# An attention block with a token and channel mixer on one core: all weight pieces converted during the attention steps, the second channel weight read back in 12 pieces

## The chip, the cores and the metric

One core of a Trainium2 chip runs the whole program. The metric is the device time of one execution in microseconds (us), and of several runs the median. The engines are called by the profile's names: PE is TensorE (PEld its weight loads), DVE is VectorE, ACT is ScalarE, POOL is GpSimd, and SP issues most of the DMA transfers.

## The reference

Windowed causal attention over 8 batches of 8 heads, followed by a mixer over tokens and a mixer over channels. Everything is float32.

```python
# q, k, v: (8, 8, 576, 64)
scores = (q @ k^T) / 8;  key position p is seen by position t if 0 <= t - p < 64
attn   = exp(scores - max) / (sum + 1e-9)
x      = (attn @ v) as (8, 576, 512)
u      = x + (relu(x^T @ w_tok1) @ w_tok2)^T      # w_tok1 (576, 256), w_tok2 (256, 576)
out    = u + relu(u @ w_ch1) @ w_ch2              # w_ch1 (512, 1536), w_ch2 (1536, 512)
```

The four weights are float64. They reach the chip as 64-bit words and are made float32 there, with integer and float operations on DVE. Products with weights are computed in three passes: each operand is split into a rounded part (hi) and a rest (lo), and hi x hi, hi x lo and lo x hi are summed.

## The kernel before

**Attention steps.** The 576 rows of each batch are cut into 9 blocks of 64. A tile holds two such blocks for all 8 heads, and there are 36 tiles, 9 to a pair of batches. The loop of lines 433 to 505 runs over i = -1 to 36 and is software-pipelined. Step i issues, in this order: the scores of tile i+1 (`qk`, L239 on PE), the transposition of the first half of tile i's probabilities (`pt_transpose`, L274 on PE, copied by ACT at L276), the mask and row maximum of the first half of tile i+1 (`softmax`, L256 and L259 on DVE), the exponentials (`softmax_exp`, L267 on ACT), a piece of the second token layer (`tok2`, L365 to L377), the second halves of the same, the first token layer for the tile before (`tok1`, L330), the value product (`av`, L286) and its normalisation (`norm`, L300 on DVE, result `x`). `split_x` then makes hi and lo of `x` on ACT and POOL for the first token layer. In the prediction, step i is the stretch from the scores of tile i+1 to those of tile i+2.

**Weight conversions.** The weights are converted in 39 jobs: 4 pieces of 320 columns of w_tok1, 3 of 384 of w_tok2, 16 of 384 of w_ch1 (jobs 7 to 22) and 16 of 384 of w_ch2 (jobs 23 to 38). A job has a load (tile `raw`, three buffers), a first half on DVE (`to_f32_a`, L162 to L164, writes `c`), a second half on DVE (`to_f32_b`, L173 to L176, writes `r`), and an addition on POOL (L178, writes `w`). `c` and `w` have two buffers, `r` has one. In the step after, `job_finish` splits the result: for w_ch1 an ACT cast to `w1hi` and a POOL subtraction to `w1lo` (L89 and L92 inside `split`). For w_ch2 it stores `w` to a scratch tensor in HBM, `w2_dram`, because the on-chip memory that w_ch2 will occupy still belongs to the attention. The table `JOBS` says how many conversions a step takes; a step that is not in it takes one, or none where i % 9 is 5. No loads are issued from step 34 on. So 33 jobs are converted in the attention steps, and the last six pieces of w_ch2 are not.

**Channel stage.** The 4608 tokens are cut into 9 chunks of 512. For chunk j the first layer computes 12 output tiles `gp` of 12 matmuls each (L549), which ACT and DVE evict as `ghi` and `glo` (L553, L554); then the second layer computes four tiles `op` of 36 matmuls (L583), adds `uf` and stores. `gp` has four PSUM tiles in turn. In chunk 0, after each output tile, `split_w2` splits a piece of w_ch2 that was read back from `w2_dram` (ACT cast to `w2hi`, POOL subtraction to `w2lo`), `load_w2` starts the next read (two buffers, pieces of 512 columns, the last of 256), and one of the six late jobs moves on: `job_finish`, `job_convert_a`, `job_convert_b` and a load.

**What sets the order.** Nothing is scheduled by a program: each engine runs its instructions in the order in which the code issues them, and the semaphores of the tile framework make them wait for data and buffers. All loads named here stand in SP's queue.

Of the kernel before, what the change touches and what calls it, by code (L numbers as in the profile page):

```python
# [10 lines left out]
F32 = mybir.dt.float32  # L11
F32R = mybir.dt.float32r
I32 = mybir.dt.int32
U32 = mybir.dt.uint32
I64 = mybir.dt.int64
# [6 lines left out]
C = H * D  # L22
P = 128
# [3 lines left out]
TPP = 9  # L27
# [4 lines left out]
NFT = F // P  # L32
# [3 lines left out]
CW = 384  # L36
# [36 lines left out]
def mixer_kernel(ctx: ExitStack, tc: tile.TileContext, qh, kh, vh, wt1, wt2, wc1, wc2, out):  # L73
    nc = tc.nc
# [12 lines left out]
    def split(eng_hi, eng_lo, hi, lo, src):  # L87
        if eng_hi is nc.scalar:
            nc.scalar.copy(hi, src)  # L89
        else:  # L90
            eng_hi.tensor_copy(hi, src)
        eng_lo.tensor_sub(lo, src, hi.bitcast(F32))  # L92
# [15 lines left out]
    with ExitStack() as actx:  # L108
# [3 lines left out]

        mask = [pa.tile([P, P], F32, name=f"mask{m}") for m in range(2)]

        kbs, loaded, cpool = {}, {}, [pq]

        def load_k(i):
            p, t = divmod(i, TPP)
# [37 lines left out]
        def to_f32_a(raw, n, tag):  # L156

            words = raw[:, :n].bitcast(I32).rearrange("p (n t) -> p n t", t=2)
            low, high = words[:, :, 0], words[:, :, 1]
            c = cpool[0].tile([P, CW], I32, name=f"c{tag}", tag="cvc", bufs=2)[:, :n]  # L160
            cf = c.bitcast(F32)
            nc.vector.tensor_scalar(out=c, in0=high, scalar1=0x7FFFFFFF, scalar2=None, op0=ALU.bitwise_and)  # L162
            nc.vector.tensor_scalar(out=cf, in0=cf, scalar1=F64_LOW, scalar2=F64_HIGH, op0=ALU.max, op1=ALU.min)
            nc.vector.tensor_scalar(out=c, in0=c, scalar1=3, scalar2=0x3FFFFFFF,  # L164
                                    op0=ALU.logical_shift_left, op1=ALU.bitwise_and)
            return c, low, high, n, tag

        def to_f32_b(c, low, high, n, tag):

            r = cpool[0].tile([P, CW], I32, name=f"r{tag}", tag="cvr", bufs=1)[:, :n]  # L170
            w = cpool[0].tile([P, CW], F32, name=f"w{tag}", tag="cvw", bufs=2)[:, :n]
            cf, rf = c.bitcast(F32), r.bitcast(F32)
            nc.vector.scalar_tensor_tensor(out=c, in0=high, scalar=-0x40000000, in1=c,  # L173
                                           op0=ALU.bitwise_and, op1=ALU.bitwise_or)
            nc.vector.tensor_scalar(out=r, in0=c, scalar1=-0x800000, scalar2=None, op0=ALU.bitwise_and)
            nc.vector.scalar_tensor_tensor(out=rf, in0=low.bitcast(U32), scalar=2.0 ** -52, in1=rf,  # L176
                                           op0=ALU.mult, op1=ALU.mult)
            nc.gpsimd.tensor_add(w, rf, cf)  # L178
            return w
# [8 lines left out]
        def job_load():  # L188
            if to_load:
                n = to_load.pop(0)  # L190
                src, _, _, o, m = jobs[n]
                raw = cpool[0].tile([P, CW], I64, name=f"raw{n}", tag="raw", bufs=3 if cpool[0] is pq else 2)
                nc.sync.dma_start(raw[:, :m], src[:, o:o + m])
                to_convert.append((n, raw))

        to_convert_b = []

        def job_convert_a():
            if to_convert:
                n, raw = to_convert.pop(0)  # L200
                to_convert_b.append((n, to_f32_a(raw, jobs[n][4], n)))

        def job_convert_b():
            if to_convert_b:
                n, part = to_convert_b.pop(0)
                to_finish.append((n, to_f32_b(*part)))
# [226 lines left out]
        for i in range(-1, NT + 1):  # L433
# [76 lines left out]
    with ExitStack() as bctx:  # L510
# [1 line left out]
        w2hi = pb.tile([P, NFT, C], F32R, name="w2hi")  # L512
        w2lo = pb.tile([P, NFT, C], F32R, name="w2lo")

        w2hf, w2lf = (t.rearrange("p f c -> p (f c)") for t in (w2hi, w2lo))
        cpool[0] = pb
        n_early = jobs[to_load[0]][3] if to_load else NFT * C
        early = [(o, min(C, n_early - o)) for o in range(0, n_early, C)]
        w2_raw = {}

        def load_w2():
            if early:
                o, m = early.pop(0)
                w2_raw[o, m] = pb.tile([P, C], F32, name=f"raww2_{o}", tag="raww2", bufs=2)
                nc.sync.dma_start(w2_raw[o, m][:, :m], w2_dram[:, o:o + m])

        def split_w2():
            if w2_raw:
                (o, m), raw = next(iter(w2_raw.items()))
                del w2_raw[o, m]  # L530
                split(nc.scalar, nc.gpsimd, w2hf[:, o:o + m], w2lf[:, o:o + m], raw[:, :m])

        load_w2()
        load_w2()
        late = list(to_load)
        while to_load and len(to_convert) < 2:
            job_load()
        for n in late:
            jobs[n] = (wc2, w2hf, w2lf) + jobs[n][3:]

        for j in range(NCHUNK):
            uf, uhi, ulo = ul.pop(j)
            g = []
            for ft in range(NFT):
                gp = ps.tile([P, CHUNK], F32, name=f"gp{j}_{ft}", tag=("s", "pt")[ft % 2])
                k = 0
                for ct in range(NCT):
                    for w, x in ((w1hi, uhi), (w1hi, ulo), (w1lo, uhi)):
                        nc.tensor.matmul(gp, w[:, ct * F + ft * P:ct * F + (ft + 1) * P], x[:, ct], start=(k == 0), stop=(k == 3 * NCT - 1))  # L549
# [4 lines left out]
                nc.vector.scalar_tensor_tensor(out=glo, in0=gp, scalar=0.0, in1=ghi.bitcast(F32),  # L554
                                               op0=ALU.max, op1=ALU.subtract)
                g.append((ghi, glo))
                if j == 0:
                    job_finish()
                    split_w2()
                    load_w2()  # L560
                    job_convert_a()
                    job_convert_b()
                    while to_load and len(to_convert) < 2:
                        job_load()
                if ft == 3 and j + 1 < NCHUNK:
                    ul[j + 1] = load_u(j + 1, pu)
                if ft == 8 and j + 1 < NCHUNK:
                    split_u(ul[j + 1])
# [56 lines left out]
```

## Time and profile before

| | us |
|---|---|
| median of 3 runs | 903.66 (903.43 to 905.66) |
| profiled execution | 901.16 |
| its span, first to last instruction | 899.2 |
| PE busy | 871.6 (97%) |
| DVE busy | 381.5 (42%) |
| ACT busy | 305.0 (34%) |
| POOL busy | 129.5 (14%) |

The attention steps with the token mixer end at 290.17 us of the span, when the first `gp` matmul's row begins; the channel stage takes the rest. The shares of busy time are averages over these two: DVE is busy nine tenths of the time in much of the attention and about two tenths in the channel stage. A matmul's end is modelled and its start overlaps the one before, so a PE that shows busy may still be held up a little, and the length of a stretch of the chain says more than its busy share. The granted TensorE clock is 0.997 on average.

### The profile page before, as it was taken

How to read it: one execution, taken by the hardware profiler on the slowest of the kernel's cores; microseconds unless marked ns; L12 is line 12 of the kernel's file. 1: busy time of each engine (PE TensorE's matmuls, PEld its weight loads, DVE VectorE, ACT ScalarE, POOL GpSimd, SP SyncE). 2: the span in 40 equal slices, each digit the busy share in tenths (PEclk: the TensorE clock that was granted, in tenths of full speed). 3: DMA queues.
4: the chain of work that ended last, by engine and by line, in shares of the span. 5: the costliest groups of instructions: out<-in, count | busy, mean ns of one | idle time of the engine just before them, and what ended most of it. 6: DMA issues, size and time to landing. Idle time of an engine off the chain costs nothing.

```text
span 899.2 us, 14591 instructions
## 1 busy us (share of the span) xinstructions
PE 871.6 (97%) x6002; PEld 704.7 (78%) x6002; DVE 381.5 (42%) x686; ACT 305.0 (34%) x953; POOL 129.5 (14%) x130
## 2 busy tenths in 40 slices
PE   7889999999999989999999999999999999999998
PEld 5667777778878768888888888888888888888887
DVE  5989979988883870130220220230220220220210
ACT  5777778787774240120120120120120220210210
POOL 2434434443331540000000000000000000000000
PEclk9999999999999999999999999999999999999999
DMA  9666668578636420100100100100100100100001
GB/s 325 183 209 237 218 216 269 184 230 293 213 124 206 113 92 36 58 1 36 59 0 36 59 1 36 58 1 36 59 12 24 59 13 23 59 12 36 0 12 36
DMA packets 41490, 87.05 MB, mean 97 GB/s; under 512 B 5456, under 2 KB 19408, under 8 KB 39504
## 3 DMA queue, kind: packets, MB, share of 16 engines
q1 hardware_dynamic: 39312, 84.29, 28.2%
q10 hardware_dynamic: 2112, 1.84, 0.6%
q8 instruction: 47, 0.77, 0.4%
q14 instruction: 19, 0.16, 0.1%
HBM read 65.27 MB, written 20.84 MB: 96 GB/s over the span
## 4 chain that ended last, share of the span: by engine, by line
PE 80%; DVE 14%; ACT 4%; issue 1%; DMA 0%; POOL 0%; SPq 0%; DVEq 0%; ACTq 0%
PE op L583 33%; PE gp L549 31%; PE up L372 4%; PE s L239 3%; PE xp L286 3%; PE h L330 3%; ACT e L267 2%; DVE nm L259 2%; DVE e L256 2%; PE up L365 2%; DVE c L173 2%; PE pp L274 1%; DVE c L162 1%; DVE c L164 1%; ACT pt L276 1%
## 5 line engine op out<-in xcount | busy, mean ns | idle before, releaser
L553 ACT ACTIVATE ghi<-gp 128x512 fp32r<-128x512 f32 x108 | 64.4, 598 | 462.6 <-PE gp L549 461.6
L549 PE MATMUL gp<-uhi,w1hi 128*128 128x512 f32 x432 | 170.5, 395 | 5.9 <-DVE glo L554 5.9
L549 PE MATMUL gp<-uhi,w1lo 128*128 128x512 f32 x432 | 172.9, 400 | 0.0
L549 PE MATMUL gp<-ulo,w1hi 128*128 128x512 f32 x432 | 171.0, 396 | 0.0
L583 PE MATMUL op<-glo,w2hi 128*128 128x512 f32 (+1 forms) x444 | 170.4, 384 | 0.0
L583 PE MATMUL op<-ghi,w2hi 128*128 128x512 f32 (+1 forms) x444 | 170.3, 384 | 0.0
L583 PE MATMUL op<-ghi,w2lo 128*128 128x512 f32 (+1 forms) x444 | 170.2, 383 | 0.0
L554 DVE SCALAR_TENSOR_TENSOR glo<-gp,ghi 128x512 fp32r<-128x512 f32 x108 | 74.4, 690 | 198.3 <-ACT ghi L553 198.2
L585 DVE TENSOR_TENSOR uf<-op,uf 128x512 f32<-128x512 f32 (+1 forms) x37 | 25.1, 677 | 262.7 <-PE op L583 262.7
L549 PEld LDWEIGHTS gp<-uhi,w1hi 128*128 128x128 f32 x432 | 81.5, 189 | 27.0 <-DVE glo L554 7.6
L267 ACT ACTIVATE e<-e,nm 128x128 f32<-128x128 f32 x232 | 90.4, 392 | 25.6 <-DVE nm L259 24.2
L549 PEld LDWEIGHTS gp<-ulo,w1hi 128*128 128x128 f32 x432 | 81.4, 188 | 20.8
L583 PEld LDWEIGHTS op<-ghi,w2hi 128*128 128x128 f32 x444 | 83.4, 188 | 16.7
L583 PEld LDWEIGHTS op<-ghi,w2lo 128*128 128x128 f32 x444 | 83.4, 188 | 16.5
L583 PEld LDWEIGHTS op<-glo,w2hi 128*128 128x128 f32 x444 | 83.4, 188 | 16.5
L549 PEld LDWEIGHTS gp<-uhi,w1lo 128*128 128x128 f32 x432 | 81.5, 189 | 18.9
L178 POOL TENSOR_TENSOR w<-r,c 128x384 f32<-128x384 f32 (+1 forms) x39 | 38.7, 993 | 142.3 <-DVE r L176 116.5
L286 PEld LDWEIGHTS xp<-v,pt 128*64 128x64 f32 x1152 | 39.4, 139 | 21.0 <-ACT pt L276 8.7
L286 PE MATMUL xp<-v,pt 128*64 128x64 f32 x1152 | 47.0, 229 | 5.8 <-ACT pt L276 5.0
L276 ACT COPY pt<-pp 128x512 f32<-128x512 f32 x72 | 41.7, 583 | 13.1 <-PE pp L274 12.8
L239 PE MATMUL s<-k,q 64*64 64x128 f32 x1152 | 43.3, 284 | 2.1 <-DVE c L173 1.6
L256 DVE SCALAR_TENSOR_TENSOR e<-s,mask 128x512 f32<-128x512 f32 x58 | 39.6, 683 | 13.2 <-PE s L239 13.1
(70 smaller groups left out, 1027.7 us busy)
## 6 DMA issues: line engine op xcount, KB each, us to landing
v<-vh SPq DMA_DIRECT2D x36, 512.0 KB, 4.2
raw<-wc SPq DMA_DIRECT2D x32, 384.0 KB, 4.5
q<-qh SPq DMA_DIRECT2D x36, 256.0 KB, 4.5
k<-kh SPq DMA_DIRECT2D x7, 1280.0 KB, 8.2
out<-uf SPq DMA_DIRECT2D x35, 256.0 KB, 2.3
uf<-u_dram SPq DMA_DIRECT2D x8, 1024.0 KB, 5.6
u_dram<-u SPq DMA_DIRECT2D x7, 512.0 KB, 4.4
w_dram<-w SPq DMA_DIRECT2D x10, 192.0 KB, 3.9
```

Of the source, the lines that this page charges most:

```text
L178: nc.gpsimd.tensor_add(w, rf, cf)
L239: nc.tensor.matmul(s[u][half * BLK:(half + 1) * BLK, j], qt[r, j, half], kbs[b][r, j, n * BLK:n * BLK + P], start=not on_pe, stop=True, sk ...
L256: nc.vector.scalar_tensor_tensor(out=e, in0=s_ps.pop((i, u)), scalar=scale, in1=mk.unsqueeze(1).to_broadcast([P, 4, P]), op0=ALU.mult, op1 ...
L267: nc.scalar.activation(e[:, h], src[:, h], AF.Exp, bias=nm[:, g:g + 1], scale=by, accum_out=sm[:, g:g + 1])
L276: nc.scalar.copy(pt, pp)
L286: nc.tensor.matmul(xp[half * BLK:(half + 1) * BLK, h], pts[h % 2][:, h // 2, half * BLK:(half + 1) * BLK], vt[:, half, h], start=True, sto ...
L330: nc.tensor.matmul(h_ps[b][tt], w[r, slot * DT + tt * P:slot * DT + (tt + 1) * P], x[r], start=first and n == 0, stop=last and n == len(co ...
L372: nc.tensor.matmul(up[:, :n], hx[:, cs], w[:, tt * S + s0:tt * S + s0 + n], start=False, stop=(k == 6), skip_group_check=True)
L549: nc.tensor.matmul(gp, w[:, ct * F + ft * P:ct * F + (ft + 1) * P], x[:, ct], start=(k == 0), stop=(k == 3 * NCT - 1))
L553: nc.scalar.activation(ghi, gp, AF.Relu)
L554: nc.vector.scalar_tensor_tensor(out=glo, in0=gp, scalar=0.0, in1=ghi.bitcast(F32), op0=ALU.max, op1=ALU.subtract)
L583: nc.tensor.matmul(op, w[:, ft, cs], x[:, cols], start=(k == 0), stop=(k == 3 * NFT - 1))
```

## The change

All 39 jobs are converted in the attention steps. `JOBS` now gives two conversions to steps 11, 16, 20, 25 and 29 and none to 34, 35 and 36; every other step takes one, also 6, 14, 23 and 32, which took none. Since the jobs run out after step 32, step 33 has none left. The late path goes: the loop that emptied the queue in step 35 becomes an assertion, and chunk 0 no longer loads, converts or finishes jobs. The conversion's tiles always come from the pool `pq`, so the list `cpool` goes too. w_ch2 comes back from `w2_dram` in 12 pieces of 512 columns instead of 7 and a half, with three buffers instead of two.

```diff
-JOBS = {-1: 1, 0: 1, 1: 1, 5: 1, 6: 0, 34: 1, 35: 1, 36: 0}
+JOBS = {11: 2, 16: 2, 20: 2, 25: 2, 29: 2, 34: 0, 35: 0, 36: 0}
...
-            n_jobs = JOBS.get(i, 1 if i % TPP != 5 else 0)
+            n_jobs = JOBS.get(i, 1)
...
             if i == NT - 1:
-                while to_convert or to_convert_b or to_finish:
-                    job_convert_a()
-                    job_convert_b()
-                    job_finish()
+                assert not (to_load or to_convert or to_convert_b or to_finish)
...
-        early = [(o, min(C, n_early - o)) for o in range(0, n_early, C)]
-        w2_raw = {}
+        w2_loads = [slice(ft, ft + 1) for ft in range(NFT)]
+        w2_raw = []
...
+                raw = pb.tile([P, C], F32, name=f"raww2_{f.start}", tag="raww2", bufs=3)
+                nc.sync.dma_start(raw, w2_dram[:, f.start * C:f.stop * C])
...
-        late = list(to_load)
-        while to_load and len(to_convert) < 2:
-            job_load()
-        for n in late:
-            jobs[n] = (wc2, w2hf, w2lf) + jobs[n][3:]
+        for _ in range(3):
+            load_w2()
...
                 if j == 0:
-                    job_finish()
                     split_w2()
                     load_w2()
-                    job_convert_a()
-                    job_convert_b()
-                    while to_load and len(to_convert) < 2:
-                        job_load()
```

How this moves instructions on DVE, at three places. First step 20, from the first half of its conversion to the normalisation. `c19` and `r19` are the tiles of job 19, `e21_1` is the masked second half of tile 21's scores, `x20` tile 20's result. Before:

```order
L162 TENSOR_SCALAR c19_2534<-raw19_2356 128x384
L163 TENSOR_SCALAR c19_2534<-c19_2534 128x384
L164 TENSOR_SCALAR c19_2534<-c19_2534 128x384
L256 SCALAR_TENSOR_TENSOR e21_1_2545<-s21_1_2486,mask0_84 128x512
L259 TENSOR_REDUCE nm21_2510<-e21_1_2545 128x4
L173 SCALAR_TENSOR_TENSOR c19_2534<-raw19_2356,c19_2534 128x384
L175 TENSOR_SCALAR r19_2558<-c19_2534 128x384
L176 SCALAR_TENSOR_TENSOR r19_2558<-raw19_2356,r19_2558 128x384
L300 TENSOR_TENSOR x20_2581<-xp20_2564,ri20_2515 128x512
```

Now, from the second job's first half on (the three rows of job 23's first half stand ahead of these):

```order
L162 TENSOR_SCALAR c24_2594<-raw24_2535 128x384
L163 TENSOR_SCALAR c24_2594<-c24_2594 128x384
L164 TENSOR_SCALAR c24_2594<-c24_2594 128x384
L256 SCALAR_TENSOR_TENSOR e21_1_2605<-s21_1_2542,mask0_84 128x512
L259 TENSOR_REDUCE nm21_2566<-e21_1_2605 128x4
L173 SCALAR_TENSOR_TENSOR c23_2590<-raw23_2412,c23_2590 128x384
L175 TENSOR_SCALAR r23_2618<-c23_2590 128x384
L176 SCALAR_TENSOR_TENSOR r23_2618<-raw23_2412,r23_2618 128x384
L173 SCALAR_TENSOR_TENSOR c24_2594<-raw24_2535,c24_2594 128x384
L175 TENSOR_SCALAR r24_2624<-c24_2594 128x384
L176 SCALAR_TENSOR_TENSOR r24_2624<-raw24_2535,r24_2624 128x384
L300 TENSOR_TENSOR x20_2647<-xp20_2630,ri20_2571 128x512
```

Three more rows stand ahead of the second half of the scores and three more ahead of the normalisation, and the two second halves follow each other directly, both writing the one buffer of `r`.

Second, step 23, from the reciprocal to the normalisation; `hlo4` is the rest part of the first token layer's result for batch 4. Before:

```order
L295 RECIPROCAL ri23_2881<-ri23_2881 128x8
L256 SCALAR_TENSOR_TENSOR e24_1_2897<-s24_1_2852,mask0_84 128x512
L259 TENSOR_REDUCE nm24_2876<-e24_1_2897 128x4
L342 SCALAR_TENSOR_TENSOR hlo4_0_2905<-h4_0_2428,hhi4_0_2904 128x512
L342 SCALAR_TENSOR_TENSOR hlo4_1_2909<-h4_1_2429,hhi4_1_2908 128x512
L300 TENSOR_TENSOR x23_2933<-xp23_2916,ri23_2881 128x512
```

Now:

```order
L295 RECIPROCAL ri23_2948<-ri23_2948 128x8
L162 TENSOR_SCALAR c27_2956<-raw27_2787 128x384
L163 TENSOR_SCALAR c27_2956<-c27_2956 128x384
L164 TENSOR_SCALAR c27_2956<-c27_2956 128x384
L256 SCALAR_TENSOR_TENSOR e24_1_2967<-s24_1_2919,mask0_84 128x512
L259 TENSOR_REDUCE nm24_2943<-e24_1_2967 128x4
L342 SCALAR_TENSOR_TENSOR hlo4_0_2975<-h4_0_2484,hhi4_0_2974 128x512
L342 SCALAR_TENSOR_TENSOR hlo4_1_2979<-h4_1_2485,hhi4_1_2978 128x512
L173 SCALAR_TENSOR_TENSOR c27_2956<-raw27_2787,c27_2956 128x384
L175 TENSOR_SCALAR r27_2986<-c27_2956 128x384
L176 SCALAR_TENSOR_TENSOR r27_2986<-raw27_2787,r27_2986 128x384
L300 TENSOR_TENSOR x23_3009<-xp23_2992,ri23_2948 128x512
```

One whole conversion has come in, its halves on both sides of the token layer's eviction.

Third, chunk 0 of the channel stage, where `glo0_2` is the rest part of output tile 2. Before:

```order
L554 SCALAR_TENSOR_TENSOR glo0_2_4559<-gp0_2_4545,ghi0_2_4558 128x512
L162 TENSOR_SCALAR c35_4568<-raw35_4508 128x384
L163 TENSOR_SCALAR c35_4568<-c35_4568 128x384
L164 TENSOR_SCALAR c35_4568<-c35_4568 128x384
L173 SCALAR_TENSOR_TENSOR c35_4568<-raw35_4508,c35_4568 128x384
L175 TENSOR_SCALAR r35_4572<-c35_4568 128x384
L176 SCALAR_TENSOR_TENSOR r35_4572<-raw35_4508,r35_4572 128x384
L554 SCALAR_TENSOR_TENSOR glo0_3_4594<-gp0_3_4580,ghi0_3_4593 128x512
```

Now:

```order
L543 SCALAR_TENSOR_TENSOR glo0_2_4609<-gp0_2_4595,ghi0_2_4608 128x512
L543 SCALAR_TENSOR_TENSOR glo0_3_4630<-gp0_3_4616,ghi0_3_4629 128x512
L543 SCALAR_TENSOR_TENSOR glo0_4_4655<-gp0_4_4641,ghi0_4_4654 128x512
L543 SCALAR_TENSOR_TENSOR glo0_5_4676<-gp0_5_4662,ghi0_5_4675 128x512
L543 SCALAR_TENSOR_TENSOR glo0_6_4697<-gp0_6_4683,ghi0_6_4696 128x512
```

The evictions follow each other with nothing between them.

More of the change, by code (lines that the diff above doesn't have):

```diff
@@ L513, in mixer_kernel @@
         w2lo = pb.tile([P, NFT, C], F32R, name="w2lo")
-        w2hf, w2lf = (t.rearrange("p f c -> p (f c)") for t in (w2hi, w2lo))
-        cpool[0] = pb
-        n_early = jobs[to_load[0]][3] if to_load else NFT * C
-        early = [(o, min(C, n_early - o)) for o in range(0, n_early, C)]
-        w2_raw = {}
-        def load_w2():
[L522 to L525, printed above, removed]
+        w2_loads = [slice(ft, ft + 1) for ft in range(NFT)]
+        w2_raw = []
+        def load_w2():
+            if w2_loads:
+                f = w2_loads.pop(0)
+                raw = pb.tile([P, C], F32, name=f"raww2_{f.start}", tag="raww2", bufs=3)
+                nc.sync.dma_start(raw, w2_dram[:, f.start * C:f.stop * C])
+                w2_raw.append((f.start, raw))
         def split_w2():
             if w2_raw:
[L529 to L534, printed above, removed]
-        late = list(to_load)
-        while to_load and len(to_convert) < 2:
-            job_load()
-        for n in late:
-            jobs[n] = (wc2, w2hf, w2lf) + jobs[n][3:]
+                f, raw = w2_raw.pop(0)
+                split(nc.scalar, nc.gpsimd, w2hi[:, f], w2lo[:, f], raw)
+        for _ in range(3):
+            load_w2()
         for j in range(NCHUNK):
```

10 lines of the change are left out of this document (5 added, 5 removed).

## The prediction

> **What bounds the kernel now.** I read the table by stretches of time first, then the chain of waits, then the timelines of VectorE (DVE) and GpSimd (POOL) where the chain leaves TensorE (PE). The table shows two stretches of the same work: the first layer of the channel stage for token chunk 0, and for chunk 1. Columns: stretch, its length, busy time of each engine (instructions), granted clock, DMA share, GB/s.
>
> ```profile
> 290.17:332.30 42.13, 36.25 (x145) 27.82 (x145) 35.09 (x49) 15.16 (x30) 22.40 (x20) 0.96 0.37 113
> 364.98:398.59 33.61, 33.61 (x145) 27.03 (x145) 10.61 (x16) 8.65 (x15) 0.00 (x0) 1.00 0.13 39
> ```
>
> The same 144 matmuls take 42.13 us in chunk 0 and 33.61 us in chunk 1, where PE has no gap. The stretches are cut where the chain enters and leaves them (start, length, what):
>
> ```profile
> 290.17 2.83 PE gp L549 x12
> ...
> 326.41 5.88 PE gp L549 x24
> 332.30 32.68 PE op L583 x144
> 364.98 33.61 PE gp L549 x144
> ```
>
> Between the first two rows the chain is on DVE. One round of DVE there:
>
> ```profile
> 303.45 0.68 DVE L554 SCALAR_TENSOR_TENSOR glo<-gp,ghi 128x512 fp32r<-128x512 f32 x1
> 304.05 0.80 DVE L162 TENSOR_SCALAR c<-raw 128x384 int32<-128x384 int32 x1
> 304.88 0.36 DVE L163 TENSOR_SCALAR c<-c 128x384 f32<-128x384 f32 x1
> ...
> 306.52 1.53 DVE L173 SCALAR_TENSOR_TENSOR c<-raw,c 128x384 int32<-128x384 int32 x1
> ...
> 309.03 0.68 DVE L554 SCALAR_TENSOR_TENSOR glo<-gp,ghi 128x512 fp32r<-128x512 f32 x1
> ```
>
> One eviction (L554) and one weight conversion (L162 to L176) make a round of 309.03 - 303.45 = 5.58 us, without a gap, while PE needs 33.61/12 = 2.80 us for an output tile. Six conversions stand there, so DVE sets the pace of that stage. In the attention steps neither engine rules alone:
>
> ```profile
> 50.00:250.00 200.00, 193.35 (x2509) 155.67 (x2507) 174.57 (x341) 157.44 (x583) 76.72 (x69) 1.00 0.69 227
> ```
>
> DVE is busy 174.57 of 200 us, and the chain passes through it, in step 20 through a conversion itself:
>
> ```profile
> 162.18 0.93 DVE c L162
> ...
> 169.57 0.87 ACT e L267 x4
> 171.28 1.03 PE xp L286 x28
> ```
>
> That is the loop that matters: a late DVE makes ScalarE's (ACT) exponentials for the next tile late, they stand ahead of the copy of the transposed probabilities in ACT's queue, and PE waits for that copy before the value product (L286). I call step i the work from the scores of tile i+1 to those of tile i+2.
>
> **What the change removes.** The six late conversions leave chunk 0. What is left per output tile is one eviction on ACT and DVE and one split of a reloaded piece, an ACT cast and a POOL subtraction. A row each of the DMA issues (last figure: us to landing), of the groups (busy us, mean ns, idle before) and of POOL's timeline:
>
> ```profile
> raww<-w_dram SPq DMA_DIRECT2D x7, 256.0 KB, 2.8
> L89 ACT CAST w2hi<-raww 128x512 fp32r<-128x512 f32 (+1 forms) x8 | 4.7, 587 | 0.0
> 306.24 1.40 POOL L92 TENSOR_TENSOR w2lo<-raww,w2hi 128x512 fp32r<-128x512 f32 x1
> ```
>
> Twelve pieces instead of eight come back. A piece holds one of three buffers for 2.8 us of transfer, 0.59 of cast and 1.40 of subtraction, 4.8 us, so a piece every 1.6 us would be possible and one every 2.80 is wanted; the 1 MB load of the next chunk in the same queue delays one or two pieces, which ACT can absorb because four PSUM tiles let PE run ahead. So chunk 0 should take chunk 1's time: **42.13 - 33.61 = 8.5 us gained**. If the reload did not keep up, that cover is gone (third rival).
>
> **What it adds.** Nine conversions enter the attention steps: one in each of steps 6, 14, 23 and 32, which had none, and a second one in steps 11, 16, 20, 25 and 29; steps 33, 34 and 35 lose theirs. A conversion unhindered, on the timelines of DVE and POOL (start, length, engine, line, operation, in brackets the idle time before it):
>
> ```profile
> 206.18 0.31 DVE L162 TENSOR_SCALAR c<-raw 128x384 int32<-128x384 int32 x1
> ...
> 207.20 0.68 DVE L256 SCALAR_TENSOR_TENSOR e<-s,mask 128x512 f32<-128x512 f32 x1
> ...
> 208.52 0.55 DVE L173 SCALAR_TENSOR_TENSOR c<-raw,c 128x384 int32<-128x384 int32 x1
> 209.17 0.36 DVE L175 TENSOR_SCALAR r<-c 128x384 int32<-128x384 int32 x1
> 209.57 0.56 DVE L176 SCALAR_TENSOR_TENSOR r<-raw,r 128x384 f32<-128x384 uint32 x1
> 210.04 0.69 DVE L300 TENSOR_TENSOR x<-xp,ri 128x512 f32<-128x512 f32 x1
> 210.27 1.02 POOL L178 TENSOR_TENSOR w<-r,c 128x384 f32<-128x384 f32 x1 [4.27 <-DVE r L176]
> ```
>
> Its first half takes 207.20 - 206.18 = 1.02 us of DVE's queue, its second half 210.04 - 208.52 = 1.52: 2.54 us. A second conversion in the same step adds a wait: tile r has one buffer, and POOL's addition (L178) must have read it before the second L175 may write it. If POOL starts as here, its addition ends 210.27 + 1.02 - 209.57 = 1.72 us after L176's start, and the second L175, due 0.47 (L176 to the next row) + 0.65 (L173 to L175) = 1.12 after it, waits 0.6. But the second L173, which has no wait, starts 0.47 after L176 and so ahead of POOL's 0.70; if POOL has to let it pass (0.55), the addition ends at 0.47 + 0.55 + 1.02 = 2.04 and the wait is 0.9. The trace shows that these two kinds of operation exclude each other: L173 took 1.53 us at 306.52, where POOL's L92 had begun at 306.24 and ran to 307.64, and 0.55 at 208.52 with POOL idle. I take 0.9, with 0.6 as the lower end. [...]
>
> So a doubled step delays DVE's normalisation (L300) by 1.02 + 1.52 + 0.9 = 3.44 us. What DVE idles just before its next eviction (L256) can swallow some of it:
>
> ```profile
> 97.67 0.69 DVE L256 SCALAR_TENSOR_TENSOR e<-s,mask 128x512 f32<-128x512 f32 x1
> 136.59 0.69 DVE L256 SCALAR_TENSOR_TENSOR e<-s,mask 128x512 f32<-128x512 f32 x1 [0.28 <-PE s L239]
> 167.25 0.68 DVE L256 SCALAR_TENSOR_TENSOR e<-s,mask 128x512 f32<-128x512 f32 x1
> 199.09 1.05 DVE L163 TENSOR_SCALAR c<-c 128x384 f32<-128x384 f32 x1
> 204.27 0.69 DVE L256 SCALAR_TENSOR_TENSOR e<-s,mask 128x512 f32<-128x512 f32 x1 [0.29 <-PE s L239]
> 234.07 0.69 DVE L256 SCALAR_TENSOR_TENSOR e<-s,mask 128x512 f32<-128x512 f32 x1 [0.61 <-PE s L239]
> ```
>
> Where no bracket is shown there was none. Step 25 also loses the stretch of L163 (1.05 against 0.36), because the w1 pieces, whose subtraction on POOL caused it, are through by step 20. Steps 11, 16, 20, 25, 29: 3.44, 3.44 - 0.28, 3.44, 3.44 - 0.29 - 0.69, 3.44 - 0.61 = 15.3 us. In the steps after 11 and 16 ACT has two w1 casts instead of one ahead of the exponentials:
>
> ```profile
> L89 ACT CAST w1hi<-w 128x384 fp32r<-128x384 f32 x16 | 8.2, 515 | 0.1
> ```
>
> 0.5 us each, 1.0 together (0 if ACT has time left). The steps that go from none to one, on the timelines:
>
> ```profile
> 59.12 0.69 DVE L300 TENSOR_TENSOR x<-xp,ri 128x512 f32<-128x512 f32 x1 [0.73 <-PE xp L286]
> 60.14 0.69 DVE L256 SCALAR_TENSOR_TENSOR e<-s,mask 128x512 f32<-128x512 f32 x1 [0.33 <-PE s L239]
> ...
> 121.16 0.69 DVE L256 SCALAR_TENSOR_TENSOR e<-s,mask 128x512 f32<-128x512 f32 x1 [1.39 <-PE s L239]
> ...
> 192.32 0.58 ACT L276 COPY pt<-pp 128x512 f32<-128x512 f32 x1
> 193.81 1.15 PE L286 MATMUL xp<-v,pt 128*64 128x64 f32 x32
> ```
>
> Step 6: 2.54 - 0.73 - 0.33 = 1.5. In steps 14, 23 and 32 DVE waits for the token layer in mid-step, which hides the first half; the second, 1.52, meets 1.39 us of idle time in step 14 (0.1 left), and in step 23 the 0.9 us between the end of ACT's copy (192.90) and PE's use of it (193.81), 0.6 left. Step 32 is the same tile of its pair, taken at the same 0.6. Together 2.8. Steps 33 to 35 give nothing back, since PE has hardly a gap there (it is busy 39.12 of the 40 us from 250 to 290); 0.4 at most. The loads of the extra raw pieces wait for no engine that is late, and the DMA share of 0.69 leaves room; 0.
>
> **Sum:** -8.5 + 15.3 + 1.0 + 2.8 = **+10.6 us**. The profiled execution took 901.16 us (span 899.2, 1.96 around it), so one like it would take 911.8; the median of the runs shown, 903.66, lies 2.5 above it, and I forecast **914.3 us**. Low end: waits of 0.6 (-1.5), no cast cost (-1.0), 0.8 less in the single steps, 0.4 back at the end, 0.2 of slack in PE's wait at each doubled step (-1.0): +5.9, 909.6. High end: a second POOL subtraction of w1 stretches DVE by another 0.69 after steps 6, 11 and 16 (+2.1), half a us less gained: +13.2, 916.9.
>
> **Rivals.** (1) *Faster: DVE's idle time swallows the conversions.* Place: steps 6 to 32. Nine conversions are 9 x 2.54 = 22.9 us, and DVE idles 200 - 174.57 = 25.4 us between 50 and 250 us. If lag can be carried over several steps until idle time comes, attention costs nothing and the 8.5 us are a clean gain: 895.2 us. It decides once attention costs under 8.5 us, 0.95 per added conversion. Against it: the value product waits on DVE's lag in the very next step, and four of the five idle times above are under 0.3 us. 6%. (2) *A draw.* Half the lag is caught up, through slack in ACT and PE that I don't see: 19.1/2 - 8.5 = +1, 904.7; 6%, of which most lies within 0.3%. (3) *The change doesn't free chunk 0*: the reload behind one queue, with the chunk load in it, paces the stage instead. At two pieces late by a transfer and a split (4.8 us each) the gain is gone: 914.3 + 8.5 = 922.8. Against it: 1.6 us against 2.80. 5%. (4) *A port war*: every added POOL operation, addition and subtraction, stretches DVE by 0.69 (1.05 against 0.36), 9 x 2 x 0.69 = 12.4 us, of which half on the path: 920.5. For it: L162 and L163 are already stretched in many steps. 8%.
>
> **How the numbers follow.** My forecast with its ends has 75%. The range takes it in and reaches a little further to both sides: 907.5 to 918.5. This kernel's runs lie up to 0.25% apart, so about 0.3%, 2.7 us, can be told from no change. Faster by more: rival 1 and a little of rival 2, 7%. Within: 5%. Slower: 88%.
>
> **What would show it.** Right: chunk 0's first layer at about 33.6 us with no conversion on DVE; attention's end some 19 us later than 290.17; the steps after 11, 16, 20, 25 and 29 two to four us longer, with PE waiting for ACT's pt copy or POOL's xlo; a gap on DVE ahead of the second L175 of a doubled step. Wrong: doubled steps longer by under 1.5 us, a chunk 0 that stays above 36 us, or gaps on PE that end on a transfer.

## The result and the profile after

| us | before | after |
|---|---|---|
| median, lowest to highest | 903.54 (901.28 to 905.66), 4 runs | 916.52 (915.86 to 918.64), 4 runs |
| profiled execution, its span | 901.16, 899.2 | 916.33, 914.3 |
| first `gp` matmul of the channel stage | 290.17 | 313.98 |

The changed kernel is slower: ratio 1.0148, 95% interval 1.0118 to 1.0178, or 13.0 us between the medians; 914.3 was forecast. The chain of waits of the changed kernel (start, length, what) shows chunk 0 without DVE:

```profile
313.98 33.61 PE gp L538 x144
347.59 32.68 PE op L567 x144
380.27 33.61 PE gp L538 x144
```

Chunk 0's first layer takes exactly chunk 1's time, 33.61 us, so 8.52 us are gained there. The attention ends 23.8 us later. Where, the starts of successive score products tell (PE timeline; the 32 matmuls of one tile are one row). Before:

```profile
203.13 1.10 PE L239 MATMUL s<-k,q 64*64 64x128 f32 x32
210.88 1.10 PE L239 MATMUL s<-k,q 64*64 64x128 f32 x32
```

and after:

```profile
218.05 1.10 PE L239 MATMUL s<-k,q 64*64 64x128 f32 x32
229.62 1.10 PE L239 MATMUL s<-k,q 64*64 64x128 f32 x32
```

This is step 26, the one after the doubled step 25: 7.75 us before, 11.57 after. Lengths are compared in this way below. In the doubled step 25 itself, on the timelines of DVE and POOL after the change (start, length, operation, in brackets the idle time ahead and what ended it):

```profile
217.47 0.55 DVE L173 SCALAR_TENSOR_TENSOR c<-raw,c 128x384 int32<-128x384 int32 x1
...
218.45 0.56 DVE L176 SCALAR_TENSOR_TENSOR r<-raw,r 128x384 f32<-128x384 uint32 x1
218.92 0.55 DVE L173 SCALAR_TENSOR_TENSOR c<-raw,c 128x384 int32<-128x384 int32 x1
220.36 0.36 DVE L175 TENSOR_SCALAR r<-c 128x384 int32<-128x384 int32 x1 [0.89 <-POOL w L178]
221.23 0.69 DVE L300 TENSOR_TENSOR x<-xp,ri 128x512 f32<-128x512 f32 x1
221.83 0.68 DVE L256 SCALAR_TENSOR_TENSOR e<-s,mask 128x512 f32<-128x512 f32 x1
...
219.14 1.19 POOL L178 TENSOR_TENSOR w<-r,c 128x384 f32<-128x384 f32 x1 [5.25 <-DVE r L176]
```

The second L175 waits for POOL as forecast. What PE's rows show next is no wait for the pt copy but two short ones in the token layer, for xhi and xlo of the late x (which of the three sets the length of the step is answered under "The place in the queue"):

```profile
222.68 0.49 PE L330 MATMUL h<-xhi,t1hi 128*128 128x512 f32 x1 [0.93 <-ACT xhi L89]
224.02 0.79 PE L330 MATMUL h<-xlo,t1hi 128*128 128x512 f32 x1 [0.85 <-POOL xlo L92]
224.61 0.63 PE L330 MATMUL h<-xhi,t1lo 128*128 128x512 f32 x1
```

The last row is new: the same matmul takes 0.63 us and elsewhere 0.40. The table of stretches has the reason in its granted clock, the third column from the right. First two pieces of step 12, then step 20's wake, then two pieces of step 26:

```profile
102.00:106.00 4.00, 1.75 (x4) 1.25 (x5) 3.90 (x8) 3.27 (x11) 3.57 (x4) 0.82 0.88 328
106.00:109.70 3.70, 3.70 (x45) 2.75 (x44) 3.49 (x7) 1.88 (x9) 0.73 (x1) 0.73 0.01 4
...
182.00:188.00 6.00, 4.98 (x55) 3.54 (x58) 5.72 (x12) 4.61 (x20) 1.71 (x2) 1.00 0.89 304
222.00:226.00 4.00, 2.48 (x6) 1.68 (x6) 3.83 (x9) 3.54 (x12) 1.71 (x2) 0.76 1.00 354
226.00:229.60 3.60, 3.60 (x43) 2.67 (x41) 2.64 (x5) 1.66 (x8) 1.00 (x1) 0.80 0.51 157
```

After steps 11 and 25 the mean clock of two neighbouring pieces is 0.73 to 0.82, after 16 and 29 the table has 0.66 to 0.90 in places; after step 20 it keeps 1.00. Behind each of these means stands one stretch of 3.41 us at half clock (a granted clock of 0.50 over each), from 104.59, 148.96, 224.06 and 258.19 us. The forecast had no such term.

### The profile page after: what moved, and what is told of

It is laid out like the page before. It is cut to its first block, busy times and chain, and to the rows that moved or that the text cites. A ratio compares the mean times of both kernels' runs of the same rounds, so it can differ in the third digit from the quotient of the medians.

```text
span 914.3 us, 14633 instructions
## 1 busy us (share of the span) xinstructions
PE 880.1 (96%) x6002; PEld 708.4 (77%) x6002; DVE 375.2 (41%) x686; ACT 304.3 (33%) x951; POOL 129.6 (14%) x128
## 4 chain that ended last, share of the span: by engine, by line
PE 70%; DVE 1%; ACT 1%; POOL 0%; issue 0%; ACTq 0%; DVEq 0%
PE gp L538 33%; PE op L567 32%; PE up L372 2%; PE up L365 1%; PE h L330 1%; PE xp L286 1%; ACT e L267 0%; PE s L239 0%; DVE nm L259 0%; DVE e L256 0%; PE pp L274 0%; POOL xlo L92 0%; DVE x L300 0%; DVE hlo L342 0%; DVE c L162 0%; DVE r L176 0%
## 5 line engine op out<-in xcount | busy, mean ns | idle before, releaser
L286 PE MATMUL xp<-v,pt 128*64 128x64 f32 x1152 | 49.2, 235 | 5.1 <-ACT pt L276 4.2
L274 PE MATMUL pp<-ident,e 128*128 128x128 f32 x288 | 45.4, 287 | 0.0
L276 ACT COPY pt<-pp 128x512 f32<-128x512 f32 x72 | 41.6, 582 | 9.9 <-PE pp L274 9.5
```

The lines of the kernel that those rows point to most:

```text
L274: nc.tensor.transpose(pp[:, h], e[:, h], ident)
L276: nc.scalar.copy(pt, pp)
L286: nc.tensor.matmul(xp[half * BLK:(half + 1) * BLK, h], pts[h % 2][:, h // 2, half * BLK:(half + 1) * BLK], vt[:, half, h], start=True, sto ...
```

## The experiments

The theory: an attention step is paced by DVE, so a conversion there costs its DVE time wherever nothing else keeps DVE waiting, while chunk 0 had room. The rivals: the wait for tile r, the drop of the clock, the token layer's waits, or the place in the queue account for it. All ratios are against the kernel before on the same chip (median there 902.7 to 903.5).

**Pricing the three parts.** The kernel `chunk_only` has the attention as before and no late conversions; a part of w_ch2 is left unconverted and other pieces read in its place.

```diff
-JOBS = {11: 2, 16: 2, 20: 2, 25: 2, 29: 2, 34: 0, 35: 0, 36: 0}
+JOBS = {-1: 1, 0: 1, 1: 1, 5: 1, 6: 0, 34: 1, 35: 1, 36: 0}
...
-            n_jobs = JOBS.get(i, 1)
+            n_jobs = JOBS.get(i, 1 if i % TPP != 5 else 0)
...
-        to_load, to_convert, to_finish = list(range(len(jobs))), [], []
+        to_load, to_convert, to_finish = list(range(33)), [], []
...
-                nc.sync.dma_start(raw, w2_dram[:, f.start * C:f.stop * C])
+                o = f.start % 7 * C
+                nc.sync.dma_start(raw, w2_dram[:, o:o + C])
```

> The changed kernel with the attention steps of the kernel before (33 conversions at its places). The six late conversions are left out altogether, and the reload reads 7 converted pieces over again for the rest, so part of w_ch2 is not the reference's. It prices the channel stage alone. If chunk 0's first layer falls to 33.6 us and nothing else moves: 903.5 - 8.5 = 895.0. If the reload in 12 pieces or the end of the attention costs something by itself: 897 or more.

Measured 894.64 (892.63 to 896.97), ratio 0.9905 (0.9889 to 0.9921), 8.9 us below the kernel before: the channel stage is worth what was forecast.

`no_doubles` has `JOBS = {34: 0, 35: 0, 36: 0}`: one conversion in every step to 32, five pieces left out in the same way.

> The changed kernel with one conversion in each of steps -1 to 32 and no second one anywhere: 34 conversions, five pieces of w_ch2 left out and read as others. Its distance to the run with the old attention is the price of the four singles less the steps 33 to 35: 2.8 by the prediction, 4.3 by the steps of the two traces. Its distance to the changed kernel is the price of the five doubles: 16.3 by the prediction's terms (15.3 and 1.0), 20.0 by the traces. So 900.2 if the prediction's terms hold, 896.5 to 899.5 if the traces' steps do.

Measured 898.31 (898.03 to 899.78), ratio 0.9948 (0.9935 to 0.9961). By the medians the doubles cost 916.52 - 898.31 = 18.2 and the singles 898.31 - 894.64 = 3.7. The medians of kernels that lose clock in different places compare badly, though; executions at full clock compare better: 892.63 (clock 1.000) for `chunk_only`, 898.04 and 898.37 (1.000) for this kernel, so 5.6 for the singles. Step by step against the trace of before, step 7 (after the single in 6) is 1.31 longer, steps 8, 9 and 10 another 0.25, 0.29 and 0.36; steps 16, 17 and 19 (after the single in 14) 0.25, 0.28 and 0.32; steps 23 and 24 together 1.25; step 33 1.32. That is 5.6 again, where 2.8 was forecast. The sums over steps 7 to 10 and 14 to 17 (columns: length, then busy PE, PEld, DVE, ACT, POOL) say why. Before:

```profile
sum 61.91, PE 60.27 PEld 48.44 DVE 52.76 ACT 49.45 POOL 23.79; mean PE 7.53 PEld 6.05 DVE 6.59 ACT 6.18 POOL 2.97
```

and with the singles:

```profile
sum 64.65, PE 61.60 PEld 48.48 DVE 61.83 ACT 49.73 POOL 27.43; mean PE 7.70 PEld 6.06 DVE 7.73 ACT 6.22 POOL 3.43
```

DVE's 9.15 us of idle time shrink to 2.82, so that little is left in which a lag could end, and the steps lengthen until the next wait on another engine. The added conversions are the smaller part of it: DVE is 9.07 us busier, but the rows that came in here (one first half, two second halves) are worth some 4.0. The rest are rows that were there before and take longer. L294 (the first step of the reciprocal, eight rows in both) goes from 3.26 to 6.17 us in sum, L162 (seven rows, then eight) from 4.28 to 8.43. In step 8, where nothing was added, DVE has before:

```profile
68.61 0.16 DVE L294 TENSOR_SCALAR ri<-sum 128x8 f32<-128x8 f32 x1
68.92 0.31 DVE L162 TENSOR_SCALAR c<-raw 128x384 int32<-128x384 int32 x1
```

and with the singles, with POOL's two subtractions beside it:

```profile
70.53 0.81 DVE L294 TENSOR_SCALAR ri<-sum 128x8 f32<-128x8 f32 x1
71.50 1.00 DVE L162 TENSOR_SCALAR c<-raw 128x384 int32<-128x384 int32 x1
...
70.03 1.29 POOL L92 TENSOR_TENSOR xlo<-x,xhi 128x512 fp32r<-128x512 f32 x1 [0.24 <-ACT xhi L89]
71.28 1.01 POOL L92 TENSOR_TENSOR w1lo<-w,w1hi 128x384 fp32r<-128x384 f32 x1
```

Both of DVE's rows now end when POOL's row beside them ends or some 0.2 us later. A lag that was small at first so made more DVE time in the steps behind it (L163 gives 0.70 us back in this step, 1.06 before and 0.36 here). This is read from the traces; no run took the collisions of the singles away.

**The wait for tile r.** `r_two` changes one number.

```diff
-            r = pq.tile([P, CW], I32, name=f"r{tag}", tag="cvr", bufs=1)[:, :n]
+            r = pq.tile([P, CW], I32, name=f"r{tag}", tag="cvr", bufs=2)[:, :n]
```

> The changed kernel with two buffers for tile r, so that the second L175 of a doubled step waits for no POOL addition. If that wait (0.8 in the trace) lies on the path in all five steps: 916.5 - 4.0 = 912.5, and 908 to 910 if the shorter lag also spares TensorE its drops of clock. If POOL and ACT, not DVE, are what TensorE waits for, or the wait moves to the buffers of c or w: 916.5.

Measured 916.09 (915.41 to 917.4), ratio 1.0142 (1.0126 to 1.0159): 0.4 us, not 4. The timelines of DVE and POOL of this kernel in step 25:

```profile
218.18 0.55 DVE L173 SCALAR_TENSOR_TENSOR c<-raw,c 128x384 int32<-128x384 int32 x1
218.77 1.04 DVE L175 TENSOR_SCALAR r<-c 128x384 int32<-128x384 int32 x1
...
218.40 1.18 POOL L178 TENSOR_TENSOR w<-r,c 128x384 f32<-128x384 f32 x1 [5.26 <-DVE r L176]
```

The bracket is gone, and L175 takes 1.04 instead of 0.36. So 0.68 of the 0.89 us was never the buffer's: L175 began at 218.77 beside POOL's addition (218.40 to 219.58) and ended at 219.81, 0.23 us behind it, though no semaphore held it.

**The clock.** `warm_pe` gives TensorE work by a tile of zeros in the token layer's waits.

```diff
                 for n, (w, x, r) in enumerate(combos):
+                    if tt == 0 and n < 2 and i in (11, 16, 20, 25, 29):
+                        for _ in range(2):
+                            nc.tensor.matmul(h_ps[b][tt], zero, t1hi[:, :C], start=False, stop=False)
```

> The changed kernel with four more 128x512 matmuls by zeros (added to h, 0.39 us each at full clock) in each step after a doubled one, two ahead of the token layer's first product and two between xhi's and xlo's, where TensorE stands still for 0.86 and 0.85 us in the trace. If the drops of the granted clock come from these gaps and cost time: no drop below 0.9, and 911 to 914. If the doubled steps are long by DVE's lag alone and the clock only shows in the records: 916.5, up to 917.5 where the zeros are longer than the gaps.

Measured 915.06 (914.09 to 916.84), ratio 1.0129 (1.0109 to 1.0149). Its PE timeline in step 26, where L335 is L330 of the changed kernel and L334 the zeros:

```profile
224.59 0.50 PE L335 MATMUL h<-xhi,t1hi 128*128 128x512 f32 x1 [0.45 <-ACT xhi L89]
224.92 0.63 PE L334 MATMUL h<-t1hi,zero 128*128 128x512 f32 x2
225.95 0.50 PE L335 MATMUL h<-xlo,t1hi 128*128 128x512 f32 x1 [0.40 <-POOL xlo L92]
226.28 0.40 PE L335 MATMUL h<-xhi,t1lo 128*128 128x512 f32 x1
```

xhi and xlo come no earlier, but the matmuls behind them take 0.40 again and not 0.63, and step 26 takes 10.38 and not 11.57. The drop costs 1.2 us in each of steps 26 and 30. That it was the zeros that kept the clock up is not shown by this one execution: `xlo_last` and `b_after` below have no zeros, and their profiled executions keep 1.00 in steps 26 and 30 too. Over four executions each the mean clock speaks for the zeros: 0.994 to 1.000 here, 0.988 to 0.994 in the changed kernel, 0.990 to 0.996 in those two. The lengths of the five steps after a doubled one:

| step | before | after | r_two | warm_pe | add_late | b_after |
|---|---|---|---|---|---|---|
| 12 | 7.17 | 11.47 | 10.64 | 10.83 | 10.64 | 10.30 |
| 17 | 7.78 | 12.55 | 12.28 | 11.77 | 11.59 | 11.14 |
| 21 | 8.06 | 11.32 | 11.13 | 11.33 | 11.16 | 10.97 |
| 26 | 7.75 | 11.57 | 11.33 | 10.38 | 9.88 | 10.10 |
| 30 | 7.75 | 11.55 | 11.63 | 10.38 | 10.49 | 10.09 |
| sum over before | 0 | 19.95 | 18.50 | 16.18 | 15.25 | 14.09 |

At full clock (914.09 and 914.23) `warm_pe` lies 16.0 above `no_doubles` at full clock, which agrees with the table's 16.18.

`add_late` adds two buffers for r to that kernel and issues both additions behind both second halves.

```diff
-            nc.gpsimd.tensor_add(w, rf, cf)
+            adds.append((w, rf, cf))
...
             for _ in range(n_jobs):
                 job_convert_b()
+            while adds:
+                nc.gpsimd.tensor_add(*adds.pop(0))
```

> The changed kernel with the zeros of the run above that kept TensorE's clock up, two buffers for r, and in a doubled step both POOL additions (L178) issued behind both second halves, so that DVE's second L173 to L176 neither wait for POOL (0.9) nor are stretched beside it (0.68 in the run with two buffers alone). If those 0.7 to 0.9 are part of what sets a doubled step: the steps after 25 and 29 at 9.5 to 9.7 us where that run had 10.38, and 911 to 912 where it had 915.1. If the two additions in a row now make POOL's subtraction for xlo late instead, or stretch the normalisation and the next eviction: 10.4 and 915.

Measured 913.27 (912.6 to 914.27), ratio 1.0108 (1.0091 to 1.0125), with 9.88 and 10.49 in the two steps. It doesn't decide what it was meant to. In its timelines of POOL and DVE in step 25 (L187 is the addition, L177 is L175):

```profile
219.61 1.19 POOL L187 TENSOR_TENSOR w<-r,c 128x384 f32<-128x384 f32 x1 [5.26 <-DVE r L178]
...
219.98 1.04 DVE L177 TENSOR_SCALAR r<-c 128x384 int32<-128x384 int32 x1
```

POOL had nothing ahead of the first addition in its queue, so a later place in the program didn't delay it, and the collision stayed. Why this kernel is still 1.8 below `warm_pe` stays open; no run here took the collision away.

**The place in the queue.** `b_after` issues the second job's second half behind the normalisation.

```diff
-            for _ in range(n_jobs):
+            for _ in range(min(n_jobs, 1)):
                 job_convert_b()
...
                     norm(i, xp, ri)
+            for _ in range(1, n_jobs):
+                job_convert_b()
```

> The changed kernel with one move: in a doubled step the second job's second half (L173 to L176, 1.52 us and the wait of 0.9) is issued behind the normalisation L300 and not ahead of it. If the doubled steps are long because what stands ahead of L300 makes the next token layer wait for x, xhi and xlo: some 2.4 us less in each, 904 to 908. If VectorE's whole work between two evictions (L256) sets the pace, wherever it stands: 916.5, less only by the waits for POOL (0.9 x 5), 912 to 916.5.

Measured 915.15 (914.17 to 917.09), ratio 1.0144 (1.0128 to 1.0161). DVE's timeline of this kernel in step 25 and at the start of 26:

```profile
217.99 0.55 DVE L173 SCALAR_TENSOR_TENSOR c<-raw,c 128x384 int32<-128x384 int32 x1
...
219.44 0.68 DVE L300 TENSOR_TENSOR x<-xp,ri 128x512 f32<-128x512 f32 x1
220.04 1.03 DVE L173 SCALAR_TENSOR_TENSOR c<-raw,c 128x384 int32<-128x384 int32 x1
221.18 0.36 DVE L175 TENSOR_SCALAR r<-c 128x384 int32<-128x384 int32 x1
...
222.05 0.68 DVE L256 SCALAR_TENSOR_TENSOR e<-s,mask 128x512 f32<-128x512 f32 x1
```

L300 now comes at once, but the next tile's L256 comes as late as ever, and that is what counts: from the first second half's L173 to that L256 it is 222.05 - 217.99 = 4.06 us here and 221.83 - 217.47 = 4.36 in the changed kernel. VectorE's work from eviction to eviction sets the pace, not the lateness of x. By itself this run does not prove that, because xlo came no earlier: on POOL the second addition, late as before, stands ahead of xlo's subtraction, and PE waits 2.02 us for xlo in step 26. The table's sum is 2.1 below that of `warm_pe`, but steps 13, 18 and 19 give 0.9, 0.6 and 0.7 back against before.

`xlo_last` puts the product with xlo last.

```diff
-                    combos = ((t1hi, xhi, full), (t1hi, xlo, full), (t1lo, xhi, full))
+                    combos = ((t1hi, xhi, full), (t1lo, xhi, full), (t1hi, xlo, full))
```

> The changed kernel with the token layer's three products in another order (hi with xhi, lo with xhi, hi with xlo), so that 0.4 us of product lie ahead of the wait for POOL's xlo, 0.85 us in the step after a doubled one and 0.2 to 0.3 elsewhere. If TensorE's wait there is on the path: 0.4 x 5 and some 0.2 in ten more steps less, 912.5 to 914.5. If VectorE's own chain through the next step sets the pace and TensorE would only wait elsewhere: 916.5.

Measured 916.33 (915.57 to 916.81), ratio 1.0147 (1.0132 to 1.0161): no change, though PE has 0.4 us more to do in each such wait. PE's timeline in step 26 says why:

```profile
227.88 1.03 PE L286 MATMUL xp<-v,pt 128*64 128x64 f32 x28 [0.32 <-ACT pt L276]
```

Now PE stands still for the pt copy, as the prediction had it. That copy sets the length of the step in the others too. Step 26, in us from its first score product (DVE's first L256 is the eviction of the next tile's scores, the copy is ACT's second L276):

| kernel | first L256 starts | pt copy ends | step ends | from the copy's end to the step's |
|---|---|---|---|---|
| before | 1.14 | 5.09 | 7.75 | 2.66 |
| warm_pe | 3.79 | 7.72 | 10.38 | 2.66 |
| xlo_last | 3.79 | 7.73 | 10.39 | 2.66 |
| b_after | 3.49 | 7.43 | 10.10 | 2.67 |
| after | 3.78 | 7.72 | 11.57 | 3.85 |

The copy ends 3.93 to 3.95 us behind the start of that eviction, and the step 2.66 or 2.67 us behind the copy; only the changed kernel, at half clock for 3.41 us of this step, takes 1.2 longer. The same 2.66, or 2.10 in other steps, stands behind the copy in steps 7 to 10, 12, 17 and 21 of these kernels wherever the clock was full. So the waits for xhi and xlo end in time, and what `b_after` gains, 0.3, is what its eviction comes earlier.

**Other places for the same work.** `tail` moves the nine conversions.

```diff
+JOBS = {6: 0, 23: 0, 32: 0, 33: 2, 34: 3, 35: 3, 36: 0}
...
-            while to_load and len(to_convert) < 2 and i < NT - 2:
+            while to_load and len(to_convert) < (3 if i >= 32 else 2) and i < NT - 1:
...
-                assert not (to_load or to_convert or to_convert_b or to_finish)
+                while to_convert or to_convert_b or to_finish:
+                    job_convert_a()
+                    job_convert_b()
+                    job_finish()
```

`c` and `w` have three buffers in it.

> All 39 conversions in the attention phase as in the changed kernel, but at other steps: none in 6, 23 and 32 and no second one up to step 32; step 14 takes one, step 33 two, 34 and 35 three each (with three buffers for c and w, loads one step longer, and the loop that empties the queue in step 35). VectorE idles 11.8 of the 20 us from 270 to 290 in the kernel before, where TensorE has no gap. If a conversion costs only where VectorE sets the pace: 894.6 (the run without late conversions) plus under 3, so 895 to 898. If three conversions in a step hold up that step's normalisation as the doubles do, or the raw loads hold up the load of u for chunk 0: 900 to 906.

Measured 914.31 (910.17 to 915.4), ratio 1.0114 (1.0094 to 1.0134). My theory, as I had applied it, was wrong here: idle time at the end of a stretch doesn't help work that stands ahead of the last normalisations. Steps 34 to 36 take 46.51 us instead of 28.60, 17.1 of them at half clock. From this kernel's timelines of DVE and PE:

```profile
279.79 0.36 DVE L175 TENSOR_SCALAR r<-c 128x384 int32<-128x384 int32 x1 [0.90 <-POOL w L178]
...
284.90 1.12 PE L274 MATMUL pp<-ident,e 128*128 128x128 f32 x4 [4.75 <-ACT pt L276]
295.98 0.80 PE L330 MATMUL h<-xhi,t1hi 128*128 128x512 f32 x1 [2.93 <-ACT xhi L89]
```

`tail_xlo` is this kernel with the other order of the products.

> The kernel with the conversions at steps 33 to 35 and, besides, the token layer's products in the order of the run above. If the wait for xlo is on the path in the ordinary steps too, 2 to 5 us less than that kernel; else the same.

Measured 915.19 (912.97 to 915.95), ratio 1.0131 (1.0114 to 1.0148): the same.

**Chunk 0 after all.** `alt` is the kernel before with fewer conversions at a time.

```diff
-                    job_convert_a()
-                    job_convert_b()
-                    while to_load and len(to_convert) < 2:
-                        job_load()
+                    if ft % 2 == 0:
+                        job_convert_a()
+                        job_convert_b()
+                        while to_load and len(to_convert) < 2:
+                            job_load()
```

> The kernel before with one edit: in chunk 0 a late conversion starts only after every second output tile, so six of them lie over 12 tiles and not over 7. Two evictions and one conversion make 5.58 + 0.68 = 6.3 us of VectorE for two tiles, TensorE needs 5.6, and four tiles of PSUM let it run ahead. If only that pace costs the 8.5 us: chunk 0's first layer at 34 to 38 us, 895 to 899.5. If the late conversions cost by their ACT casts and POOL subtractions or hold up the second layer's last pieces: 901 to 904.

Measured 898.38 (897.16 to 899.48), ratio 0.9949 (0.9935 to 0.9963). Its chain of waits, one round:

```profile
300.82 0.69 DVE glo L554
...
305.84 1.03 POOL w L178
306.89 1.04 ACT w2hi L89 x2
...
308.45 0.69 DVE glo L554
```

A round of 7.63 us for two tiles: the ACT cast of a job waits for POOL's addition, and the next eviction stands behind it. `alt2` therefore moves `job_finish()` into the same branch, ahead of `job_convert_a()`, and calls it once more after the last tile.

> The kernel before with a late conversion after every second output tile of chunk 0, and its finish (ACT cast, POOL subtraction) issued two tiles later, just ahead of the next conversion, so that ACT's cast no longer stands waiting for POOL's addition ahead of the next eviction, as it did in the run with every second tile (898.4). If that wait held its rounds at 7.6 us for two tiles: rounds of 5.6 to 6.3, 894.5 to 897. If VectorE's own 6.3 and the split of the next chunk pace it: 898.

Measured **894.30 (893.41 to 894.56), ratio 0.9904 (0.9892 to 0.9917)**. Its chain:

```profile
290.34 8.43 PE gp L549 x36
...
304.72 1.28 DVE glo L554 x2
...
311.49 1.20 DVE glo L554 x2
...
331.97 25.23 PE op L585 x110
357.20 33.61 PE gp L549 x144
```

Rounds of 6.77 us, more than PE's 5.6, so DVE is still the chain; but 34 of the second layer's 144 matmuls are done by 331.97, and chunk 0 takes 357.20 - 290.34 = 66.9 us over both layers, against 74.8 before and 66.3 after the change. The six conversions stay in chunk 0 for 0.6 us; in the attention they cost the changed kernel the whole gain and more. It beats both kernels and equals `chunk_only`, which leaves the six conversions out.

`alt3` also takes two conversions back into the attention: `JOBS = {5: 1, 6: 0, 14: 1, 36: 0}` and loads one step longer.

> As the run above, and two of the six late conversions go back into the attention phase: one into step 14, where VectorE waits 1.39 us in mid-step, one behind the last normalisation in step 35, where it waits 3.8 us for the token layer's last eviction. Four are left in chunk 0. If conversions are free where VectorE waits: 0.5 to 2 us less than the run above. If the one in step 35 holds up the last token layer or the load of u: 1 to 3 us more.

Measured 899.40 (896.77 to 902.57), ratio 0.9963 (0.9950 to 0.9976), 5.1 above `alt2`: the direction of the expectation's last case, and more of it. Steps 34 to 36 are 2.0 us longer, and steps 23 and 24, which got no conversion, 1.5: they hold 3.41 us of half clock, from 192.01. Its profiled execution also had the drop of the clock in step 6 that is told of in the last section.

## Why the prediction was right, and where not

- **Chunk 0, -8.5: right.** 33.61 us in the trace, 8.9 by medians. No reload paced it (third rival).
- **Doubled steps with the w1 casts, +16.3: right in sum, and in kind.** 16.2 by the steps of `warm_pe`, single steps within 0.33: 3.66, 3.99, 3.27, 2.63, 2.63 against the 3.94, 3.66, 3.44, 2.46, 2.83 of its terms. The wait of 0.9 for the second L175 was 0.89 in the rows, but `r_two` shows that it is the running beside POOL's addition more than the buffer: without the wait L175 took 1.04 us instead of 0.36. Nor do these rows show the two kinds of operation excluding each other, as the reckoning had it: the addition began at 219.14, within L173's row (218.92 to 219.47), L173 took its 0.55 and the addition 1.19 instead of 1.02. The path held as well: DVE's next eviction comes late, the exponentials behind it, the pt copy behind them, and the step ends some 2.66 us after that copy (the table of step 26). The waits for xhi and xlo, the most visible gaps on PE, are not what counts: neither an earlier x (`b_after`) nor a later xlo product (`xlo_last`) changed the time by more than 1.4 us. The 0.5 us for the second w1 cast were 0.4 each: from the eviction to the copy's end it is 4.33 and 4.38 us in steps 12 and 17, 3.93 and 3.98 before.
- **Missing: the clock.** 19.95 - 16.18 = 3.8 us in the profiled execution, some 1.5 by the medians of `warm_pe`.
- **Singles, +2.8: the step that failed.** 5.6 in `no_doubles`. The prediction set the unhindered length of a conversion against idle time and slack. In steps 23 and 32 the slack of 0.9 ahead of PE's use of the pt copy was there (0.96 and 0.97), but the first half was not hidden: its L162 took 1.39 and 1.25 us beside a POOL subtraction (L312) instead of 0.31, the next step's first L256 came 2.45 and 2.28 late, and 1.25 and 1.32 were left where 0.6 was forecast. The 1.39 us of idle time in step 14 were counted as cover that leaves 0.1, but with them went the slack of the following steps, which lengthened by 0.85. Step 6 at 1.5 was 1.31 and 0.9 more in the three steps after, where L294 and L162 ran longer beside POOL (0.81 and 1.00 us in step 8, 0.16 and 0.31 before).
- **Steps 34 to 36 giving nothing back: right**, 28.60 us in both traces.
- The sum by these runs at full clock is -8.4 + 5.6 + 16.0 = 13.2 (the first is 892.63 against the lowest of the executions before, 900.8 to 901.2), the measured distance 13.0: the forecast of 10.6 was low by the singles. The first rival fell with `no_doubles` and `tail`. The fourth, the port war, was right in kind: beside POOL's rows DVE's took longer (those of step 8 by 0.65 and 0.69 us), and that is part of the singles' 5.6; that it is a port which the two share was not shown; the 6.2 us that it put on the path would have given 920.5.

## What to carry to other kernels

Before work is moved to where an engine is "only" nine tenths busy, count the idle time that ends each lag there: here DVE's, 9.15 us over the eight steps summed above, fell to 2.82, those steps grew by 2.74 us (61.91 to 64.65), and the lag that stayed moved other instructions beside the work of another engine, where they took longer (L294 0.81 us instead of 0.16). Where an engine paces a stretch of one stage and is busy for two tenths of the time in the rest of it, the same work is first to be tried there in a slower rhythm: `alt2` got the whole gain by every second tile and by putting the cast behind the eviction that it held up. Before a buffer that is waited for is doubled, see how long its writer takes beside its reader: the second buffer for r took a wait of 0.89 us away and brought 0.4 us in the whole kernel, since L175 took 1.04 us beside the addition instead of 0.36.

## What the runs showed of the hardware

In these traces TensorE's clock fell behind surprisingly short pauses. Two pauses of 0.93 and 0.85 us in step 26, with PE busy 2.48 of 4 us, were followed by half clock (a mean of 0.76 in these 4 us); a pair of 0.86 and 0.84 in step 21 left it at 1.00, and one pause of 2.02 us in `b_after` too (its stretch from 222.50 to 226.00: busy 1.48 of 3.50, clock 1.00). In the changed kernel half clock begins at 53.39, 104.59, 148.96, 224.06 and 258.19 us and lasts 3.41 us each time; these starts lie 15, 13, 22 and 10 times 3.413 us apart (204.80 us in 60 such pieces). In `tail` a drop lasts 6.83 us and in `chunk_only` one lasts 13.65, two and four times as long. So in the trace of the changed kernel the clock changed only at the marks of a grid of 3.413 us, and in `chunk_only` the marks lay elsewhere (the first, counted back, is 2.19 us behind the span's start here, 1.04 there). How long PE was busy in the piece of the grid ahead did not decide alone: 1.64 us (220.65 to 224.06) were followed by half clock here, 1.64 (220.87 to 224.28) by full clock in `b_after`. The largest drop is in steps 5 and 6, 13.65 us from 48.83 in `chunk_only` (a granted clock of 0.50 from 51 to 57 us, 1.00 in before), and comes in some executions only. The same stretch in the profiled execution of `chunk_only`, whose attention is that of before:

```profile
57.00:63.00 6.00, 6.00 (x37) 3.65 (x39) 1.64 (x3) 3.42 (x17) 0.00 (x0) 0.54 0.00 0
```

and before:

```profile
57.00:63.00 6.00, 6.00 (x90) 5.12 (x89) 4.76 (x11) 5.04 (x21) 1.29 (x1) 1.00 0.41 111
```

At half clock a 128x512 matmul takes 0.63 us, 0.79 behind a pause (0.40 and 0.50 at full clock), and step 6 takes 11.86 us instead of 8.23: 3.6 us that no edit accounts for, and most of the distance between two executions of one kernel (`chunk_only`: 892.63 at a mean clock of 1.000, 896.97 at 0.992). Whether a drop hangs on where a pause happens to fall on this grid was not shown.
